# A written instruction order, half as many start-up products of ones and a reordered first batch in a packed-attention and ELU feed-forward kernel

## Chip, core and metric

The kernel runs on one core of a Trainium2 chip. The metric is device microseconds of one execution; the time before is the median of 3 runs. The engines are TensorE (PE; its weight loads are PEld), VectorE (DVE), ScalarE (ACT), GpSimd (POOL) and SyncE (SP), which here only issues DMAs.

## What is computed

Eight batches of eight heads attend twice through 32 packed rows per head, and the result goes through a feed-forward layer with ELU:

```python
def sm_attn(qq, kk, vv):
    s = scale * np.matmul(qq, kk.transpose(0, 1, 3, 2))
    s = s - np.max(s, axis=-1, keepdims=True)
    a = np.exp(s)
    a = a / (np.sum(a, axis=-1, keepdims=True) + 1e-09)
    return np.matmul(a, vv)
p_packed = sm_attn(p, k, v)
out = sm_attn(q, p_packed, p_packed)
...
h = x @ w_in
g = np.where(h > 0.0, h, alpha * (np.exp(np.minimum(h, 0.0)) - 1.0))
return (g @ w_out).astype(np.float32)
```

Here q, k and v are 8 x 8 x 576 x 64, p is 8 x 8 x 32 x 64, w_in is 512 x 2048, w_out is 2048 x 512, and x is the attention output as 4608 tokens of 512.

## The kernel before, in words

**Attention of a batch.** `attention(b, ts)` loads packed rows p, keys, values and queries. `s1` (L588) multiplies keys by p; `smax1` and `sexp1` (L599, L605) are the first softmax; `tr1` (L695) transposes its result on TensorE and four copies by the helper of L377 bring it back; `pv` (L721) multiplies it by the values, 40 small products for both groups of heads (g = 0 and 1); `norm` (L733) divides, `tr2` (L747) transposes, `tr2c` copies: that is ppT, the packed values. `s2` (L770) multiplies ppT by the queries, in two halves of 288 tokens. The second softmax is then a chain of steps over 128 x 576 elements of one half: `fold` (L778), `smax`, `ssub`, `sexp` (on ScalarE), `ssum`, `srec`, `smul`, `unfold` (L822). Its result is called a.

**Feed-forward.** The attention output is never formed: `mstep` (L886) multiplies ppT by w_in into a matrix m (copied from PSUM by the L377 helper as m_hi, its remainder m_lo by L899), and h = a times m. For the first batch's first 512 columns of w_in this product is plain float32 (L1420); elsewhere it is three products of high and low parts (L1427, L1146). Then ELU, a split of the result into g (cast on L377, remainder by L1469 or L1237), and the product with w_out (L1542 to L1545 in batches 0 and 1; L1306 in later batches, where pairs of blocks are combined by sums on L1228 first, so that fewer products are needed). The weights arrive in 64-bit words: a load `raw` (L408), a cast `tops` (L377), a `join` (L426), and for w_out a split in high and low. Four `raw` buffers go round.

**What sets the order.** Every piece of work is an `op` with a priority, the engines that may do it with a cost each, dependences and buffers. `schedule()` (L220) walks a clock of its own over those costs and grants engines and buffers; the order in which it grants them is the order in which instructions are written, so each engine runs its queue in exactly that order. `Ring` and `Banks` say when buffers and PSUM banks come free. `FIRST` (L101) orders the first loads.

**Products of ones.** `warm_up` (L380) multiplies a tile of ones into a PSUM bank nobody reads. It runs with `N_WARM` = 14 (L107) ahead of everything, 20 more `op`s of two can fill idle time (`N_FILL`, L108), and `schedule()` puts further ones behind a TensorE op where the clock shows a gap, up to the first dense product. 63 run in all, 22 of them ahead of `s1`.

**The end.** Accumulators of the last two blocks are added into the tiles kvq and part on VectorE (L1338) and stored.

## Time and profile before

| | |
|---|---|
| median of 3 runs | 659.95 us (659.65 to 660.55) |
| profiled execution, first to last instruction | 657.06 us |
| median less that span | 2.89 us |
| PE busy | 646.5 us, 98% of the span |
| DVE, ACT, POOL busy | 513.0, 421.5, 99.0 us |
| DMA, whole span | 140.50 MB, mean 214 GB/s |

The times are of whole executions; the profile has one execution's span, and no time of its own for what lies around it. A timeline row reads: start, length, engine and line, operation, output and input tiles, shapes, count, and in brackets how long the engine was idle before and what ended that. TensorE's products are pipelined, so "busy" there means that products are in flight.

### The profile page before, as it was taken

How to read it: one execution, taken by the hardware profiler on the slowest of the kernel's cores; microseconds unless marked ns; L12 is line 12 of the kernel's file. 1: busy time of each engine (PE TensorE's matmuls, PEld its weight loads, DVE VectorE, ACT ScalarE, POOL GpSimd, SP SyncE). 2: the span in 40 equal slices, each digit the busy share in tenths (PEclk: the TensorE clock that was granted, in tenths of full speed). 3: DMA queues.
4: the chain of work that ended last, by engine and by line, in shares of the span. 5: the costliest groups of instructions: out<-in, count | busy, mean ns of one | idle time of the engine just before them, and what ended most of it. 6: DMA issues, size and time to landing. Idle time of an engine off the chain costs nothing.

```text
span 657.1 us, 15842 instructions
## 1 busy us (share of the span) xinstructions
PE 646.5 (98%) x6049; PEld 571.1 (87%) x6049; DVE 513.0 (78%) x1083; ACT 421.5 (64%) x839; POOL 99.0 (15%) x133
## 2 busy tenths in 40 slices
PE   9999999999999999999999999999999999999996
PEld 4567888898789989898998997999989998999996
DVE  2878755999988897767986768758997778778885
ACT  4798898777775666655675555765566567555451
POOL 1245466211210010000201000001110002000000
PEclk9999999999999999999999999999999999999999
DMA  8896761787949666583678484547867155775873
GB/s 334 320 334 214 268 234 46 214 248 216 259 138 303 214 210 211 183 252 133 224 253 280 127 255 127 165 129 250 274 225 240 47 169 170 221 229 178 302 228 129
DMA packets 88108, 140.50 MB, mean 214 GB/s; under 512 B 24544, under 2 KB 34272, under 8 KB 87776
## 3 DMA queue, kind: packets, MB, share of 16 engines
q1 hardware_dynamic: 86304, 136.34, 63.7%
q0 software_dynamic: 1440, 2.62, 2.4%
q8 instruction: 48, 0.79, 0.5%
q10 hardware_dynamic: 288, 0.52, 0.2%
q14 instruction: 28, 0.23, 0.1%
HBM read 114.81 MB, written 24.64 MB: 212 GB/s over the span
## 4 chain that ended last, share of the span: by engine, by line
PE 90%; ACT 4%; DVE 4%; issue 1%; DVEq 0%; ACTq 0%
PE psum L1306 42%; PE psum L1146 22%; PE psum L1427 5%; PE psum L886 4%; PE psum L1542 3%; PE psum L1545 3%; PE psum L1543 3%; PE psum L384 2%; PE psum L721 1%; PE psum L770 1%; PE psum L695 1%; PE psum L1420 1%; ACT tops L377 1%; ACT e L1445 1%; ACT e L1451 1%
## 5 line engine op out<-in xcount | busy, mean ns | idle before, releaser
L1306 PE MATMUL psum<-sw,g 128*128 128x256 f32 x936 | 132.7, 276 | 0.0
L1306 PEld LDWEIGHTS psum<-sw,g 128*128 128x128 f32 x936 | 118.3, 192 | 1.9 <-issue 0.8
L1237 DVE TENSOR_TENSOR g<-w,g 128x896 fp32r<-128x896 f32 (+1 forms) x96 | 91.1, 950 | 26.8 <-ACT g L377 26.1
L1146 PE MATMUL psum<-a_hi,m_hi 128*128 128x256 f32 (+1 forms) x384 | 111.6, 291 | 0.1
L1146 PE MATMUL psum<-a_lo,m_hi 128*128 128x256 f32 (+1 forms) x384 | 110.2, 287 | 0.0
L1146 PE MATMUL psum<-a_hi,m_lo 128*128 128x256 f32 (+1 forms) x384 | 110.2, 287 | 0.0
L377 ACT CAST g<-w 128x896 fp32r<-128x896 f32 (+1 forms) x96 | 78.4, 821 | 48.5 <-PE psum L1306 21.2
L1306 PE MATMUL psum<-wo_b,g 128*128 128x256 f32 (+1 forms) x675 | 106.5, 298 | 0.0
L1306 PEld LDWEIGHTS psum<-wo_b,g 128*128 128x128 f32 x675 | 93.4, 191 | 6.1 <-issue 2.2
L1306 PE MATMUL psum<-wo_a,g 128*128 128x256 f32 (+1 forms) x591 | 95.8, 297 | 0.0
L1306 PEld LDWEIGHTS psum<-wo_a,g 128*128 128x128 f32 x591 | 81.3, 191 | 8.7 <-issue 4.4
L1146 PEld LDWEIGHTS psum<-a_hi,m_hi 128*128 128x128 f32 x384 | 73.2, 191 | 3.6 <-issue 0.9
L1146 PEld LDWEIGHTS psum<-a_lo,m_hi 128*128 128x128 f32 x384 | 73.3, 191 | 0.5
L1158 ACT ACTIVATE e<-psum 128x320 f32<-128x320 f32 x96 | 41.4, 432 | 49.9 <-PE psum L1146 49.0
L1146 PEld LDWEIGHTS psum<-a_hi,m_lo 128*128 128x128 f32 x384 | 73.2, 190 | 0.0
L1153 DVE SCALAR_TENSOR_TENSOR w<-e,psum 128x256 f32<-128x256 f32 x96 | 40.0, 416 | 28.4 <-ACT e L1161 27.8
L1228 POOL TENSOR_TENSOR w<-w 128x128 f32<-128x128 f32 (+1 forms) x41 | 23.3, 568 | 248.9 <-DVE w L1153 117.8
L1158 ACT ACTIVATE w<-psum 128x512 f32<-128x512 f32 x48 | 28.7, 599 | 43.6 <-PE psum L1146 28.6
L1228 DVE TENSOR_TENSOR w<-w 128x256 f32<-128x256 f32 (+1 forms) x145 | 49.4, 341 | 2.2
L1161 ACT ACTIVATE e<-e 128x320 f32<-128x320 f32 x96 | 45.0, 471 | 2.6
L1153 DVE SCALAR_TENSOR_TENSOR w<-w,psum 128x512 f32<-128x512 f32 x48 | 32.5, 678 | 15.7 <-ACT w L1161 15.3
L899 DVE TENSOR_TENSOR m_lo<-psum,m_hi 128x1024 fp32r<-128x1024 f32 (+1 forms) x38 | 37.7, 1015 | 2.7 <-ACT m_hi L377 2.6
(123 smaller groups left out, 1188.1 us busy)
## 6 DMA issues: line engine op xcount, KB each, us to landing
sw<-sw_dram SPq DMA_DIRECT2D x248, 256.0 KB, 3.9
kvq<-in_v SPq DMA_DIRECT2D x16, 512.0 KB, 5.2
sw_dram<-sw SPq DMA_DIRECT2D x32, 256.0 KB, 3.9
raw<-in_w_out SPq DMA_DIRECT2D x16, 511.8 KB, 5.3
raw<-in_w_in SPq DMA_DIRECT2D x16, 511.8 KB, 5.7
kvq<-in_kT SPq DMA_DIRECT2D x14, 576.0 KB, 5.3
kvq<-in_qT SPq DMA_DIRECT2D x14, 576.0 KB, 5.5
out<-part SPq DMA_DIRECT2D x28, 256.0 KB, 3.8
```

The source lines that it names most:

```text
L377: (nc.scalar.copy if e == "ACT" else nc.vector.tensor_copy)(out=out, in_=in_)
L886: nc.tensor.matmul(ps.t[cols_of(pair), g, :w], lhsT=st.ppT.t[rows_of(g), pair, :], rhs=w_in_sb[rows_of(g), pair, c * FC + part * w:c * FC ...
L899: nc.vector.tensor_tensor(out=m_b[1].t[:, :, fs], in0=ps.t[:, :, :w], in1=m_b[0].t[:, :, fs].bitcast(F32), op=ALU.subtract,)
L1146: nc.tensor.matmul(ps, lhsT=m_b[p].t[:, g, o:o + P], rhs=in_turn(st.a.t[q][:, g, cols]), start=(n == 0), stop=(n == 3 * G - 1),)
L1153: nc.vector.scalar_tensor_tensor(out=out, in0=e_, scalar=-1.0, in1=ps, op0=ALU.add, op1=ALU.max)
L1158: nc.scalar.activation(out=out, in_=ps, func=AF.Relu, scale=-1.0)
L1161: nc.scalar.activation(out=x, in_=x, func=AF.Exp, scale=-1.0)
L1228: eng(e).tensor_tensor(out=out, in0=x, in1=y, op=o)
L1237: nc.vector.tensor_tensor(out=g_b.all[:, 7 * P:(7 + b1 - b0) * P], in0=blocks(b0, b1), in1=g_b.all[:, :(b1 - b0) * P].bitcast(F32), op=ALU ...
L1306: nc.tensor.matmul(a.t[:, at * H:(at + rhs.shape[1]) * H], lhsT=operand(blk, p), rhs=rhs, start=new and n == k == 0, stop=a.final == (u, m ...
L1427: nc.tensor.matmul(ps_b.t[:, :n_tok], lhsT=m_b[x].t[:, g, o:o + P], rhs=in_turn(st.a.t[y][:, g, cols]), start=(n == 0), stop=(n == 3 * G - 1),
L1542: nc.tensor.matmul(a.t, lhsT=g_b.t[0][:, t], rhs=w[0], start=first, stop=False)
```

## The change

1. **First loads.** The p of batch 0 is issued from ScalarE's queue. The queries of batch 0 come in two loads, of 256 and 320 tokens. `FIRST` names keys, values, first queries, then weights; the written order decides in the end.
2. **Products of ones.** `N_WARM` is 11, `N_FILL` 0, and a table `ONES` says how many follow which op: 13 ahead of `s1`, 36 in all. The memset of the ones covers half the tile and stands first on VectorE.
3. **Value product.** In batch 0 `pv` is two ops, one for each head group, each waiting for its own two copies.
4. **Second softmax.** In batch 0 its two parts are of 256 and 320 tokens, not 288 and 288, and the first waits for the first query load alone.
5. **A written order.** `schedule()`, `Ring.grant` and `Banks.places` are gone. `ORDER` lists all ops with an engine letter where there is a choice, and `PLACES` the PSUM bank of each; dependences stay and are still waited for. Costs given to `op` change too, but no longer decide anything.

```diff
+ORDER = """
+2 1 7 416 417A 0 8 9 10 14 11 403 404V 405 12 17 13 15A 16A 18A 3 4 19A 20 400 5 22A 418 21 23V 24
+25A 408 401V 402 26 406V 6 27 28 29 409A 410 37 407G 48 55 529 30 31 424 425A 32 33 34 426 530A 733
...
+PLACES = (
+    "462626066252064324016426346264562456720412121043201162304343030040371030416061024640015621523016"
...
+ONES = {0: 2, 8: 7, 21: 1, 26: 7, 529: 8}
...
+    CUTS = slice(0, 2 * P), slice(2 * P, S)
...
-    FIRST = "k o0 i1 o1 q v i0 i2 i3".split()
+    FIRST = "k0 v0 v1 q0 i0 i1 q1 o0 i2 i3 o1".split()
...
-    N_WARM = 14
-    N_FILL = 20
+    N_WARM = 11
+    N_FILL = 0
...
-    def schedule():
...
+    nc.vector.memset(part_sb[:, 0, :E // 2], 1.0)
     nc.vector.memset(ebias, -1023.0 * LN2)
...
-    nc.vector.memset(part_sb[:, 0, :], 1.0)
...
-                nc.sync.dma_start(out=q_b[0].t, in_=qT[b])
+                cs = CUTS[n]
+                nc.sync.dma_start(out=q_b[0].t[:, :, cs], in_=qT[b, :, :, cs])
...
-            nc.sync.dma_start(out=p_b.t, in_=pT[b])
+            (nc.sync if b else nc.scalar).dma_start(out=p_b.t, in_=pT[b])
...
-        o = op(ts[2], {"PE": 1.19}, pv, ld_v + tr_done, take=[ps, pp_b], use=v_b + e1T, mode=2)
+        if b == 0:
+            o = op(
+                ts[2], {"PE": 0.65}, lambda e: pv(e, [0]), ld_v + tr_done[:2], take=[ps, pp_b],
+                use=v_b + e1T[:1], mode=2,
+            )
+            pvs = [o, op(
+                ts[2], {"PE": 0.65}, lambda e: pv(e, [1]), tr_done[2:], use=[ps, pp_b] + v_b + e1T[1:],
+                mode=2, after=[o],
+            )]
...
+            cs = CUTS[half] if b == 0 else slice(half * HS, (half + 1) * HS)
+            w = cs.stop - cs.start
...
     with tc.manual_schedule():
-        for o, e in schedule():
+        for x in ORDER.split():
+            o = ops[int(x.rstrip("PVAG"))]
+            e = on_name[x[-1]] if x[-1] in on_name else next(iter(o.on))
+            assert e in o.on and seen.issuperset(d.n for d in o.deps + o.after)
+            seen.add(o.n)
             for buf in o.take:
+                if isinstance(buf.ring, Banks):
+                    buf.at = int(next(places))
                 buf.t = buf.make()
             o.fn(e)
-            if o.ones > 0:
-                warm_up(e, o.ones)
+            if o.n in ONES:
+                warm_up(e, ONES[o.n])
```

The order moves instructions all over the program. Three places follow, each as it stood and as it stands. The first is SyncE's queue from its first load on; k0 and q0 are the first batch's keys and queries, kvq its values, raw a weight, p packed rows.

```order
L560 DMA p_132<-in_pT 128x128
L533 DMA k0_134<-in_kT 128x2304
L408 DMA raw_141<-in_w_out 128x2047
L408 DMA raw_165<-in_w_in 128x2047
L408 DMA raw_173<-in_w_out 128x2047
L542 DMA kvq_185<-in_v 128x2x512
L546 DMA kvq_185<-in_v 64x256
L542 DMA kvq_205<-in_v 128x2x512
L546 DMA kvq_205<-in_v 64x256
L552 DMA q0_220<-in_qT 128x2304
L408 DMA raw_274<-in_w_in 128x2047
L408 DMA raw_292<-in_w_in 128x2047
```

After the change the same stretch of SyncE's queue reads:

```order
L583 DMA k0_118<-in_kT 128x2304
L458 DMA raw_123<-in_w_in 128x2047
L458 DMA raw_175<-in_w_out 128x2047
L592 DMA kvq_193<-in_v 128x2x512
L596 DMA kvq_193<-in_v 64x256
L592 DMA kvq_196<-in_v 128x2x512
L596 DMA kvq_196<-in_v 64x256
L458 DMA raw_221<-in_w_in 128x2047
L603 DMA q0_223<-in_qT 128x4x256
L458 DMA raw_252<-in_w_in 128x2047
L603 DMA q0_223<-in_qT 128x4x320
L611 DMA p_290<-in_pT 128x128
```

Packed rows leave this queue; three weights that stood ahead of the values become two; the queries are cut, and their first 256 tokens stand behind three weights, as the whole did, one of which now follows the values. In both kernels the second batch's keys come behind the same loads: all of the first batch, the same six weights, and that batch's p.

The second is ScalarE, from the copy of the first batch's packed values (ppT) to the first cast of a. tmp is the second softmax's tile, where ACTIVATE is its exponential; m_hi is the first part of m.

```order
L377 COPY ppT_277<-psum_95 128x128
L377 CAST wo_a_107<-mi_272 128x512
L377 CAST tops_114<-raw_274 128x512
L377 CAST tops_114<-raw_292 128x512
L796 ACTIVATE tmp_283<-tmp_283 128x576
L377 CAST tops_114<-raw_308 128x512
L377 COPY m_hi_328<-psum_95 128x2x256
L377 CAST a_hi_363<-k0_355 128x2x288
```

After the change ScalarE reads, between the same two:

```order
L427 COPY ppT_249<-psum_95 128x128
L427 CAST tops_114<-raw_252 128x512
L866 ACTIVATE tmp_256<-tmp_256 128x512
L427 CAST tops_114<-raw_313 128x512
L427 COPY m_hi_293<-psum_95 128x2x256
L427 CAST a_hi_326<-k0_319 128x2x256
```

Two casts ahead of the exponential become one, and one of the last weights stands between the exponential and m_hi in both.

The third is VectorE at the end of the kernel: the last additions into part and kvq.

```order
L1338 TENSOR_TENSOR part_85<-part_85,psum_95 128x256
L1338 TENSOR_TENSOR part_85<-part_85,psum_95 128x2x256
L1338 TENSOR_TENSOR kvq_8877<-kvq_8877,psum_95 128x256
L1338 TENSOR_TENSOR part_85<-part_85,psum_95 128x256
L1338 TENSOR_TENSOR part_85<-part_85,psum_95 128x512
L1338 TENSOR_TENSOR part_85<-part_85,psum_95 128x256
```

After the change VectorE ends with:

```order
L1411 TENSOR_TENSOR part_85<-part_85,psum_95 128x256
L1411 TENSOR_TENSOR part_85<-part_85,psum_95 128x2x256
L1411 TENSOR_TENSOR part_85<-part_85,psum_95 128x256
L1411 TENSOR_TENSOR kvq_8845<-kvq_8845,psum_95 128x256
L1411 TENSOR_TENSOR part_85<-part_85,psum_95 128x512
L1411 TENSOR_TENSOR part_85<-part_85,psum_95 128x256
```

The addition into kvq, which waits for TensorE's last products, stood ahead of three additions into part and stands ahead of two.

On TensorE the second batch's `s1` stands, in both kernels, between the first two blocks' products h and the next two blocks'; it stood behind the second part of m and now stands ahead of it. Elsewhere the counts change by engine: of the 234 block sums (L1228) POOL did 53 and does 126, VectorE did 181 and does 108. The number of products on TensorE other than ones is the same, and so is the number of changes between products of different tile sizes, 140.

## Rows read from the trace of the kernel before

**Rows 1.** Stretches: length, busy PE, PEld, DVE, ACT, POOL; PE clock, DMA share, GB/s

```profile
0.00:25.20 25.20, 22.91 (x234) 9.85 (x234) 10.54 (x19) 12.01 (x24) 5.24 (x11) 1.00 0.94 358
25.20:40.00 14.80, 13.13 (x193) 9.78 (x194) 12.87 (x25) 13.77 (x33) 5.18 (x5) 1.00 0.81 273
40.00:60.00 20.00, 19.98 (x187) 14.00 (x186) 16.04 (x33) 18.87 (x44) 11.47 (x12) 1.00 0.91 302
...
100.00:650.00 550.00, 549.87 (x5157) 503.20 (x5156) 443.61 (x948) 341.75 (x659) 57.60 (x84) 1.00 0.65 202
```

**Rows 2.** TensorE timeline, first 30 us: start, length, work, idle before it

```profile
1.48 7.58 PE L384 MATMUL psum<-part 128*128 128x512 bf16 x22 [1.48 <-DVE part L332]
8.99 1.20 PE L588 MATMUL psum<-k,p 64*32 64x288 f32 x32
...
13.29 2.32 PE L384 MATMUL psum<-part 128*128 128x512 bf16 x10
15.54 1.46 PE L721 MATMUL psum<-kvq,tmp 128*32 128x64 f32 x80
...
18.21 1.20 PE L770 MATMUL psum<-q,ppT 64*32 64x288 f32 x32
...
25.24 1.96 PE L1420 MATMUL psum<-k,m_hi 128*128 128x256 f32 x8 [0.40 <-DVE k L822]
...
27.59 1.18 PE L588 MATMUL psum<-kvq,p 64*32 64x288 f32 x32
29.07 1.97 PE L1420 MATMUL psum<-k,m_hi 128*128 128x256 f32 x8 [0.30 <-DVE e L1454]
```

**Rows 3.** DMA view, 1 to 22 us: queues, issues, KB, us to landing

```profile
q8 instruction: 1, 0.02, 0.3%
...
k<-in_kT SPq DMA_DIRECT2D x1, 1152.0 KB, 5.2
q<-in_qT SPq DMA_DIRECT2D x1, 1152.0 KB, 9.9
```

**Rows 4.** DMA view, 3.3 to 22 us: mean rate while the queue is full

```profile
DMA packets 2204, 7.54 MB, mean 403 GB/s; under 512 B 223, under 2 KB 479, under 8 KB 1966
```

**Rows 5.** SyncE timeline, first 42 us: when loads are issued

```profile
1.18 0.42 SPq L533 DMA_DIRECT2D k<-in_kT  x1
...
6.41 0.35 SPq L552 DMA_DIRECT2D q<-in_qT  x1
```

**Rows 6.** Tile raw, issues from 5 to 7.9 us: first load behind the queries

```profile
L408 SPq DMA_DIRECT2D raw<-in_w_in x1: 340/340/340, 7.7 to 7.7; - x1
...
DMA to landing us min/median/max: 11.4/11.4/11.4
```

**Rows 7.** Tile in_kT, issues from 16 to 20 us: second batch's keys

```profile
L535 SPq DMA_DIRECT2D kvq<-in_kT x2: 328/644/960, 17.0 to 17.5; - x2
...
DMA to landing us min/median/max: 6.2/6.7/7.2
```

**Rows 8.** VectorE timeline: first step of batch 0's second softmax

```profile
19.11 0.78 DVE L778 STREAM_TRANSPOSE tmp<-psum 128x576 f32<-128x576 f32 x1 [1.90 <-PE psum L770]
```

**Rows 9.** ScalarE timeline: a weight cast, then the copy the product needs

```profile
22.11 0.78 ACT L377 CAST tops<-raw 128x512 f16<-128x512 bf16 x1
22.90 0.59 ACT L377 COPY m_hi<-psum 128x512 f32<-128x512 f32 x1
```

**Rows 10.** Instructions by line and form, VectorE: block sums

```profile
L1228 DVE TENSOR_TENSOR w<-w 128x128 f32<-128x128 f32 x91 | 26.6, 293 | 1.4
```

**Rows 11.** Instructions by line and form, POOL: block sums

```profile
L1228 POOL TENSOR_TENSOR w<-w 128x128 f32<-128x128 f32 x33 | 16.5, 500 | 223.0 <-DVE w L1153 117.8 <-DVE hb L1153 72.4 <-DVE w L1228 32.5
```

**Rows 12.** Tile w on line 1228 of POOL: shortest, median and longest sum

```profile
L1228 POOL TENSOR_TENSOR w<-w x41: 455/460/1362, 187.4 to 610.9; 128x128 f32<-128x128 f32 x33, 128x256 f32<-128x256 f32 x8
```

**Rows 13.** VectorE timeline, end of the kernel: the last additions

```profile
651.40 0.42 DVE L1338 TENSOR_TENSOR kvq<-kvq,psum 128x256 f32<-128x256 f32 x1
651.73 1.34 DVE L1338 TENSOR_TENSOR part<-part,psum 128x256 f32<-128x256 f32 x3
```

More of the change, by code (lines that the diff above doesn't have):

```diff
@@ L153, in __init__ @@
         def __init__(self, n):
-            self.n, self.taken = n, []
-        def grant(self, bufs, now):
-            for k in range(len(self.taken) - self.n, len(self.taken) - self.n + len(bufs)):
-                if k >= 0 and not self.taken[k].released(now):
-                    return False
-            return True
-        def take(self, bufs, now):
-            self.taken += bufs
-    class Banks:
-        def __init__(self, n):
-            self.held = [None] * n
-        def places(self, bufs, now):
-            free = [h is None or h.released(now) for h in self.held]
-            out = []
-            for b in bufs:
-                at = [i for i in range(0, min(len(free), b.lim), b.n) if all(free[i:i + b.n])]
-                if not at:
-                    return None
-                i = min(at, key=lambda i: (free[i ^ 1], i)) if b.n == 1 else at[-1]
-                free[i:i + b.n] = [False] * b.n
-                out.append(i)
-            return out
-        def grant(self, bufs, now):
-            return self.places(bufs, now) is not None
-        def take(self, bufs, now):
-            for b, i in zip(bufs, self.places(bufs, now)):
-                b.at = i
-                self.held[i:i + b.n] = [b] * b.n
+            self.n = n
+    class Banks(Ring):
+        pass
     class Buf:
@@ L192, in __init__ @@
             self.ring, self.make, self.n, self.users, self.t = ring, make, n, [], None
-            self.free, self.lim = False, 8
-        def released(self, now):
-            self.free = self.free or all(u.end is not None and u.end <= now for u in self.users)
-            return self.free
+            self.at, self.lim = None, 8
     class Op:
@@ L451, in weights @@
         last = op(
-            prio, {"DVE": 0.69}, join, [x], take=take if plain or first else [mi_b],
+            prio, {"DVE": 0.73}, join, [x], take=take if plain or first else [mi_b],
             use=[raw, top_b] + [b for b in words_b if b not in take],
@@ L559, in load_p @@
         def load_p(e):
[L560 removed]
+            (nc.sync if b else nc.scalar).dma_start(out=p_b.t, in_=pT[b])
         lds, prev_ld = {}, prev_b and prev_b.ld_q
[L563 removed]
+        ld_p = op(ts[0] - 6 if b else -1000, {"DMA": 0.3} if b else {"ACT": 0.45}, load_p, take=[p_b], after=[prev_ld], lag=1.5)
         for name, fn, bufs, t in (
@@ L910, in mstep @@
         ready = mstep_done(b, c, part, parts_, prio, ps, m_b, hi, lo_, whole)
-        ready(op(prio, {"PE": 0.86 / parts_}, mm, pre, after=[b >= NB0 and m_last[0] or None],
+        ready(op(prio, {"PE": 0.89 if parts_ == 1 else 0.46}, mm, pre, after=[b >= NB0 and m_last[0] or None],
                  take=[ps] + (m_b if part == 0 else []), use=[st.ppT] + (m_b if part else []), mode=1))
@@ L1365, in strassen_pair @@
             q = i - T_SE
-            y = op(q, {"ACT": 0.45} | ({} if both else {"DVE": 0.4}), first, [acc[0].last], take=[part], use=acc[:1])
+            y = op(q, {"ACT": 0.375} | ({} if both else {"DVE": 0.425}), first, [acc[0].last], take=[part], use=acc[:1])
             y = op(q, {"DVE": 0.42}, add1, [y], use=[part, acc[0]])
```

376 lines of the change are left out of this document (233 added, 143 removed), and 3 rows, old and new, of the table ORDER.

## The prediction

> **What bounds the kernel now.** I read the stretches first [rows 1], for the engine that never rests. From 100 to 650 us TensorE is busy 549.87 of 550.00 us: nothing is to be won there without fewer products, and the change removes none. From 25.2 to 40 us it idles 14.80 - 13.13 = 1.67 us, from 40 to 60 us 0.02 us. The first 25.2 us are another matter: the TensorE timeline [rows 2] shows no dense product before 25.24 us, only the first batch's attention with products of ones between. So each microsecond by which that first dense product comes earlier shortens the kernel, if what follows can keep up.
>
> What held the start? In the timeline the 22 ones run from 1.48 us for 7.58 us, and the product of keys follows at 8.99 with no idle time. The keys were issued at 1.18 and landed 5.2 us later, at 6.4 [rows 3, 5]: the ones held `s1` for 2.6 us. The ten ones at 13.29 likewise run up to the value product at 15.54. The queries were issued at 6.41 and landed 9.9 us later, at 16.3 [rows 3, 5], yet `s2` began at 18.21: attention, not the load, was late. Loads are close behind, though: from 3.3 to 22 us the queue moves 403 GB/s without a pause [rows 4], which is 524,288 / 403,000 = 1.30 us for a piece of 512 KB.
>
> The sum is made against the profiled span, 657.06 us; the 2.89 us to the median of 659.95 are taken as unchanged.
>
> **Part by part.**
>
> *Ones ahead of `s1`.* 22 in 7.58 us, against ten in 2.32 us later [rows 2]. At a late pace of 0.215 us, 22 would take 4.7; the excess of 2.85 is 13 or 14 products at twice that, 0.43. Their spacing is that of 1.2 GHz, then of 2.4 GHz. The 13 that stay take 13 x 0.43 = 5.5 us. The half-size memset, now first, starts them some 0.35 us earlier (0.1 us for the other memset, 0.25 us for half of the ones), so at 1.1 us, and `s1` can start at 6.65 instead of 8.99.
>
> *First loads.* The keys are now SyncE's first load: one issue earlier, 0.45 us (an issue takes 0.42 [rows 5]), so they land at 5.95. The first 256 tokens of the queries stand behind the same three weights as the whole did, but need 640 KB less: 16.3 - 0.45 - 640/512 x 1.30 = 14.2 us. The p load goes to ScalarE's queue, which then has nothing else to do; it costs its 64 KB of the same transfer time, 0.16 us.
>
> *Value product in two.* `s1` to `pv` was 6.55 us with ones between; without the ten ones' 2.3 us it would be about 4.3, so 11.0 us. The values, at 5.95 + (512 + 512 + 1152)/512 x 1.30, land at 11.5 to 12. From `pv` to `s2` it was 18.21 - 15.54 = 2.67. With the first group's norm beside the second group's product, `s2` would start at 14.0 to 14.4. Both sides meet: I take **`s2` at 14.2 us**, 4.0 earlier.
>
> *256 tokens first.* The chain from its first step to the dense product was 25.24 - 19.11 = 6.13 us [rows 2, 8]. Seven passes of 0.78 us over 576 elements lose 64 of them, at most 0.09 us each, so 0.5 us; `s2` to the first step loses 0.1. The dense product could start at 14.2 + 0.8 + 5.6 = 20.6 us.
>
> *What is late next.* First ScalarE: it must cast a weight, then copy m_hi (0.78 and 0.59, [rows 9]), and that weight (i3) comes late. Before, the first 512 KB behind the queries were issued at 7.7 and landed 11.4 us later, at 19.1 [rows 6], though 16.3 + 1.30 = 17.6 would do. One packet of instructions moved on another queue between 1 and 22 us [rows 3]; I read the 1.5 us as one DMA engine held up by it. The second batch's keys, issued at 17.5, landed 7.2 later, at 24.7 [rows 7], with the same delay. After the change the same loads stand ahead of those keys, so they land at 24.7 - 0.45 = 24.2, or at 22.7 without the delay. The weight i3 would land at about 20.1 or 18.6, and the dense product start at 21.5 or 20.6. Four products h take 1.96 us; then TensorE meets `s1` of batch 2, whose keys are in at 24.2: it waits 0.7 us or more. It ran at 27.59. **This wait ends last**, so of the earlier start 27.59 - 24.2 = 3.4 us remain. Its bounds are 2.3 (if the m copy behind it also slips: the next products h at 26.8 for 29.07) and 4.6 (no delay).
>
> *25 to 100 us.* The 1.67 us of waits [rows 1] stand on ScalarE, VectorE and weights. The order is new there, and what it waits for cannot be read from the trace of before. All of it may go, or as much may come; weights have the DMA time, since the queue was busy 0.81 of 25 to 40 us. I take half gone, 0.8, with bounds of 1.7 gained and 1.7 lost.
>
> *The end.* TensorE's last products release an addition into kvq at 651.40, and the three into part last from 651.73 for 1.34 us [rows 13]. One of the three, 0.33 us from start to start, now stands ahead of that wait: 0.3 us saved.
>
> *Sums on POOL.* 73 more of them, at 0.50 us against VectorE's 0.29 [rows 10, 11]. 73 x 0.5 = 37 us more on POOL, which has 57.6 of 550 busy; VectorE has 443.6 of 550. I cost it at nothing: TensorE's full queue covers it, as long as each g is ready before its turn; without cover it costs the 0.21 us difference or more a sum. POOL's sums, of both widths, took 0.46 us in the median and up to 1.36 [rows 12]; I read the long ones as held up by VectorE. The Trainium skill (SBUF — State Buffer, Who interferes with whom) says that a VectorE instruction with two SBUF inputs and a GpSimd one that reads SBUF exclude each other, the later one waiting for the whole of the other; that speaks against this change. By that rule VectorE would lose up to 37 us of waiting and 73 x 0.29 = 21 us of work: 459 of 550, still not the bound, and the sum stays.
>
> Sum: 3.4 + 0.8 + 0.3 = 4.5 us, so 659.95 - 4.5 = **655.4 us**.
>
> **Rivals.**
> - *Loads without the delay, waits gone.* The held-up DMA engine is hit later, the dense part starts 4.6 us earlier, 1.5 of the waits go, 0.3 at the end: 653.5. For it: 27 ones are fewer, so TensorE's instruction packets come later. Against: one such packet in 20 us suffices.
> - *Conversion gives it back.* From 25.2 to 60 us ScalarE is busy 32.64 of 34.80 us [rows 1]. If it is the pace, only its 2.2 us of free time can be saved, and 0.3 at the end: 657.5. Against: several casts and copies go to VectorE, which has 5.9 us free.
> - *POOL makes g late: slower.* Each sum moved lengthens its chain by 0.21 us, and by up to 1.36 - 0.29 = 1.07 where it is blocked. With 73 at a mean of 0.2, some 15 us of lengthening stand against the lead that g has on TensorE. It decides where over 4.5 us of it, a third, outlast that lead; with half, 655.4 + 7.3 = 662.7. Against: TensorE never idled from 100 to 650 us [rows 1].
> - *Clock.* The granted clock is 1.00 (2.4 GHz) in every stretch from 25.2 us [rows 1], with ones in each gap; now 27 ones go and gaps of about a microsecond are left. A fall to 1.2 GHz before the dense part costs what it cost at the start, 13 x 0.215 = 2.8 us: 658.2. The Trainium skill (TensorE: Matmul & The Clock Gate, Part 1) says that idleness puts the clock back to half; no gap here shows it yet.
> - *Nothing much happens.* If the second batch's keys come late by another 3 us, the start is worth nothing: about 659.5.
>
> **How the numbers follow.** Chances: forecast (654.2 to 656.8) 0.47, no delay 0.17, conversion 0.15, POOL 0.09, clock 0.05, nothing 0.07. A measurement tells 0.2%, 1.3 us, from no change, so faster means under 658.6. That holds for the first two, nearly all of the third and most of the fourth case: 0.81. The same: 0.10; slower: 0.09. The range leaves out the POOL case and the upper part of the last, and below goes 0.9 us under the second case for its bounds: 652.6 to 658.6.
>
> **What would show it.** Right: `s1` near 6.7 us, `s2` near 14.2, first dense product at 20.6 to 21.5, `s1` of the second batch at about 24.2 right behind its keys, last addition within 1.5 us of TensorE's end. Wrong: `s1` of the second batch near 27; TensorE idle by more than 2 us from 25 to 100; idle time from 100 to 650 us released by g or by POOL; a granted clock under 1.00 after the start.

## The result, and the profile after

The changed kernel takes 663.41 us (median of 4 runs, 662.81 to 664.2), the kernel before 659.8 us beside it (4 runs, 658.61 to 660.55): ratio 1.0059, 95% interval 1.0044 to 1.0073. It is **slower by 3.6 us** where the prediction had it 4.5 us faster. The profiled execution took 663.94 us, with a span of 662.2.

The stretches of [rows 1], now of the changed kernel (length, busy PE, PEld, DVE, ACT, POOL; PE clock, DMA share, GB/s):

```profile
0.00:25.20 25.20, 21.25 (x237) 9.69 (x245) 13.45 (x27) 11.35 (x24) 3.90 (x10) 0.93 0.96 357
25.20:40.00 14.80, 13.87 (x207) 10.47 (x191) 14.46 (x29) 13.01 (x30) 8.21 (x7) 1.00 0.88 302
40.00:60.00 20.00, 18.41 (x162) 12.81 (x161) 19.93 (x38) 17.39 (x36) 8.29 (x9) 1.00 0.76 258
60.00:100.00 40.00, 37.62 (x256) 31.86 (x255) 37.02 (x78) 31.20 (x69) 13.49 (x13) 1.00 0.61 198
100.00:650.00 550.00, 547.57 (x5127) 498.34 (x5125) 432.49 (x865) 334.31 (x640) 132.51 (x175) 1.00 0.65 205
```

The engine that never rests is now VectorE: 19.93 of 20.00 us from 40 to 60, 37.02 of 40 behind. TensorE, which stood still for 0.02 us from 40 to 60 and 0.13 from 100 to 650 [rows 1], stands still for 1.59 and 2.43 us. POOL's time behind 100 us has gone from 57.60 to 132.51 us.

TensorE's timeline, as [rows 2]:

```profile
1.18 4.88 PE L434 MATMUL psum<-part 128*128 128x512 bf16 x13 [1.18 <-DVE ebias L380]
7.21 1.20 PE L643 MATMUL psum<-k,p 64*32 64x288 f32 x32 [1.15 <-POOL p L710]
...
11.59 2.08 PE L776 MATMUL psum<-kvq,tmp 128*32 128x64 f32 x80
...
15.23 1.11 PE L837 MATMUL psum<-q,ppT 64*32 64x256 f32 x16 [0.67 <-DMA q<-in_qT]
16.27 2.88 PE L434 MATMUL psum<-part 128*128 128x512 bf16 x7
19.55 0.77 PE L837 MATMUL psum<-q,ppT 64*32 64x320 f32 x16 [0.40 <-DMA q<-in_qT]
...
22.42 1.89 PE L1493 MATMUL psum<-k,m_hi 128*128 128x256 f32 x8
24.24 1.58 PE L643 MATMUL psum<-kvq,p 64*32 64x288 f32 x28
...
27.43 1.99 PE L1493 MATMUL psum<-k,m_hi 128*128 128x256 f32 x8 [0.93 <-ACT m_hi L427]
```

The first dense product (L1493, before L1420) starts at 22.42 for 25.24, the second batch's `s1` (L643) at 24.24 for 27.59. Not all of that is gain: this `s1` now runs ahead of the second part of m, which took 0.46 us of TensorE before it (27.13 to 27.59). The next products h are the first place where both kernels have the same work behind them. They start at 27.43 for 29.07, after a wait for the m_hi copy: there **1.6 us** of the head's gain are left.

**Where the lead goes.** The span shows only the end, so I compared the two traces product by product. Each TensorE `op` starts at a known time in each trace; the table costs of the ops started before it, summed, say how far the program is; the two times at equal progress differ by the lead. Left, the time in the kernel before; minus means ahead, in us. Every column is one profiled execution; e1 and e2 are the runs with engines put back, low_v, f_lows and so on those described under the same names below.

```
time   after  e1    e2   low_v f_lows f_sp f_ones f_all  m75  m180  m520 best520 sumsG best150 best434
  28   -3.5  -3.9  -2.1  -2.1  -2.3  -3.9  -4.1  -3.9  -2.1  -3.4  -3.9  -3.8  -4.0  -3.6  -3.4
  44   -4.0  -1.9  -2.6  -2.5  -2.6  -4.3  -4.5  -4.2  +1.8  -3.8  -4.3  -4.2  -4.3  -4.3  -3.7
  60   -2.0  -0.6  -0.6  -1.7  -1.8  -2.2  -2.5  -3.4  +1.8  -0.5  -2.1  -2.8  -3.4  -0.1  -1.9
  84   -2.2  +3.2  -0.9  -1.9  -1.9  -2.4  -2.7  -3.6  +1.8  -0.1  -2.3  -3.0  -3.6  -0.3  -2.1
 102   +0.2  +6.5  +0.3  +0.5  -1.3  -0.4  -1.5  -2.9  +1.8  +0.1  +0.2  -1.7  -2.1  +0.4  +1.0
 147   +0.9  +7.4  +1.0  +1.2  -0.6  +0.3  -1.0  -2.2  +2.9  +0.1  +4.1  +2.1  +1.9  +1.5  +1.0
 291   +2.3  +7.8  +3.2  +2.5  +0.8  +3.5  +0.4  -1.7  +3.0  +0.2  +4.2  +2.4  +3.2  +1.5  +1.1
 578   +3.1  +7.9 +13.9  +2.8  +1.2  +4.0  +0.8  -0.2  +3.0  +0.6  +4.2  +2.4  +4.5  +1.8  +1.3
 638   +4.2  +8.9 +15.9  +3.6  +2.5  +4.1  +0.9  -0.1  +3.0  +0.6  +4.4  +2.4  +5.4  +1.9  +1.3
```

The first row stands inside the swapped `s1` and m, so it reads too high. Where both kernels have started exactly the same products, the changed kernel is ahead by 2.8 us at the first dense product, 1.6 at 29 us, 2.3 at 36, 3.5 at 42, 1.6 at 44 and 82, and behind by 0.9 at 105 and 4.8 at the last product. The table's later rows are some 0.6 us more favourable than that, and their falls are the same within 0.3 us. So the changed kernel gains 1.6 us in its head and some 2 more by 42 us, where waits of the kernel before are gone; it gives back 4.2 us between 44 and 102 us and 4.0 us more behind. The columns e2, low_v, f_lows and m75 start lower for the clock's sake (*Ones and the clock*). (The span grew by 5.1 us, the medians by 3.6: the profiled execution of after was one of its slower ones, that of before, as far as its span tells, one of its quicker ones.) The longest waits of TensorE, without those of the first 20 us (waits: who waited for whom; us in total, times, longest):

```profile
PE psum L837 <- DVE w_in_sb L476: 1.6, 1, 1.6
PE psum L1500 <- DVE e L1527: 1.3, 2, 0.8
...
PE psum L1379 <- DMA sw<-sw_dram: 1.0, 2, 0.8
```

No wait is long. I had three theories: **V**, VectorE took over work of ScalarE and GpSimd in 25 to 100 us and is the pace there; **S**, the sums of g on GpSimd cost the time behind 100 us; **W**, it is the written order itself, whatever the engines. A fourth, **B**, came from the trace: VectorE and GpSimd keep each other waiting.

### The profile page after: what moved, and what is told of

Read it like the earlier page. It is cut to its first block, busy times and chain, and to the rows that moved or that the text cites. A ratio compares the mean times of both kernels' runs of the same rounds, so it can differ in the third digit from the quotient of the medians.

```text
span 662.2 us, 15833 instructions
## 1 busy us (share of the span) xinstructions
PE 644.9 (97%) x6022; PEld 569.2 (86%) x6022; DVE 523.4 (79%) x1045; ACT 408.4 (62%) x797; POOL 166.4 (25%) x213
## 4 chain that ended last, share of the span: by engine, by line
PE 77%; DVE 10%; DMA 6%; ACT 3%; issue 2%; SPq 1%; DVEq 0%; ACTq 0%
PE psum L1379 40%; PE psum L1219 21%; PE psum L959 4%; PE psum L1500 3%; DMA raw<-in_w_in 2%; DMA sw<-sw_dram 2%; PE psum L1615 2%; PE psum L1618 2%; PE psum L1616 2%; DVE e L1527 1%; PE psum L776 1%; DMA kvq<-in_v 1%; DVE w_in_sb L476 1%; PE psum L837 1%; ACT tops L427 1%
## 5 line engine op out<-in xcount | busy, mean ns | idle before, releaser
L1301 POOL TENSOR_TENSOR w<-w 128x128 f32<-128x128 f32 (+1 forms) x104 | 75.3, 727 | 327.8 <-DVE w L1226 137.8
L1379 PE MATMUL psum<-wo_a,g 128*128 128x256 f32 (+1 forms) x591 | 93.9, 295 | 0.0
L1231 ACT ACTIVATE e<-psum 128x320 f32<-128x320 f32 x96 | 41.5, 432 | 61.6 <-PE psum L1219 58.6
L1226 DVE SCALAR_TENSOR_TENSOR w<-e,psum 128x256 f32<-128x256 f32 x96 | 38.4, 415 | 15.5 <-ACT e L1234 15.2
L1542 POOL TENSOR_TENSOR g<-e,g 128x256 fp32r<-128x256 f32 x34 | 29.7, 879 | 47.3 <-DVE g L427 24.1
```

What stands on the lines that cost most here:

```text
L1226: nc.vector.scalar_tensor_tensor(out=out, in0=e_, scalar=-1.0, in1=ps, op0=ALU.add, op1=ALU.max)
L1231: nc.scalar.activation(out=out, in_=ps, func=AF.Relu, scale=-1.0)
L1301: eng(e).tensor_tensor(out=out, in0=x, in1=y, op=o)
L1379: nc.tensor.matmul(a.t[:, at * H:(at + rhs.shape[1]) * H], lhsT=operand(blk, p), rhs=rhs, start=new and n == k == 0, stop=a.final == (u, m ...
L1542: eng(e).tensor_tensor(out=g_b.t[1], in0=e_b.t[:, own], in1=g_b.t[0].bitcast(F32), op=ALU.subtract)
```

## Experiments

In the diffs, an entry of `ORDER` is an op's number and a letter for its engine: V VectorE, A ScalarE, G GpSimd.

**Engines put back.** First the two edits that leave the order and change engines only.

```diff
+BACK = """
+63A 64A 69A 111A 414A 422A 468A 478A 479G 486A 492A 494A 495G 511G 518A 519G 526A 527G 751A 758A
+766G 818A 835A 856G 862A 863G 869A 870G 877G 883A 884G 890A 891G 898G 904A 917G 926G 933A 950A
+"""
...
+        back = {x[:-1]: x for x in BACK.split()}
         for x in ORDER.split():
+            x = back.get(x.rstrip("PVAG"), x)
```

> The changed kernel's written order as it stands, but 39 of its entries between 25 and 100 us go back to the engine that they have in the kernel before: casts (top, high, cast, norm, tr1a, tr1b) from VectorE to ScalarE, subtractions (low, sub_own) from VectorE to GpSimd. Theory V (VectorE took over some 12 us of ScalarE's and GpSimd's work in 25 to 100 us and became the pace there; the changed kernel's lead of 3.5 us at 44 us is gone at 100): 660.0 to 661.5, and the lead at 100 us is 2 us or more. Rival S (the sums of g on GpSimd, later, are the loss): 663.4, no change. Rival W (it is the order, not the engine; in an order written for other engines the work then waits elsewhere): 663 or slower.

Measured: 668.68 us, ratio 1.0154 (1.0127 to 1.0182): 5.3 us slower than the changed kernel by the medians, 6.3 by the ratios. From 60 to 100 us VectorE falls to 23.77 us, yet TensorE stands still for 3.99:

```profile
60.00:100.00 40.00, 36.01 (x240) 29.88 (x238) 23.77 (x45) 33.05 (x75) 19.86 (x22) 1.00 0.57 183
```

Its longest waits from 25 to 104 us end on ScalarE now:

```profile
PE psum L1504 <- ACT tops L431: 1.4, 1, 1.4
PE psum L780 <- ACT tmp L431: 1.2, 1, 1.2
PE psum L963 <- ACT tmp L664: 1.1, 1, 1.1
```

That is rival W's range: V, as "the engines were chosen badly", is out; in this order VectorE is the better place for that work. The other edit is the same with 129 sums in `BACK` (`1300V 1316V 1317V ...`).

> The changed kernel with the 129 sums of g that changed their engine put back on the engine of the kernel before (101 from GpSimd to VectorE, 28 the other way), nothing else. Theory V: 663.4, since nothing changes ahead of 100 us. Rival S: from 100 us on the changed kernel loses about 3.4 us against the kernel before, and its GpSimd has 132 us of work there for 58; if the sums are that loss, 660 to 661.5. If the written order alone loses it: 663 to 665.

Measured: 676.05 us, ratio 1.0257 (1.0235 to 1.0279), 12.6 us slower. The lead falls from -0.9 at 84 us to +15.9, most of it behind 291 us; no expectation reaches so far. The longest waits from 140 us on are for VectorE's ELU (L1237), in whose queue 73 more sums now stand:

```profile
PE psum L1230 <- DVE w L1237: 4.0, 5, 2.3
PE psum L1390 <- DVE w L1237: 1.2, 2, 0.7
```

S, as a fault that one could undo, is out too. In this order both groups of engine choices are better than those of the kernel before.

**The old planner behind the new head.** `schedule()`, `Ring` and `Banks` of the kernel before are back, with most of its costs; the first entries are forced, 75 of them in the first run and 480 in the second.

```diff
+HEAD = """
+2 1 7 416 417A 0 8 9 10 14 11 403 404V 405 12 17 13 15A 16A 18A 3 4 19A 20 400 5 22A 418 21 23V 24
...
+"""
...
+            for n, o in enumerate([head[len(out)][0]] if len(out) < len(head) else todo[:400]):
...
-        for x in ORDER.split():
+        for o, e in schedule():
```

> The changed kernel's code and the first 75 entries of its written order (to 27 us: loads, ones, first attention, first dense products), then the kernel before's planner with its costs for the rest. If the head's gain of 3.3 us is real and everything behind it (engines, order) gives it back: 655.5 to 657. If the gain can't survive, since the conversion of weights holds the pace whatever the order: 659 to 660.5.

> The same with the first 480 entries (to 100 us), then the planner. Theory V and a second loss behind 100 us of about 3.4 us: as far as 100 us it is the changed kernel (level with the kernel before), from there the kernel before: 659.3 to 660.5. If everything is lost ahead of 100 us and no order can mend it: 663. If the first 100 us cost nothing: 656 to 657.

Measured: 675.55 us (1.0244, 1.0222 to 1.0266) and 669.41 us (1.0163, 1.0143 to 1.0183). Both miss every expectation. The planner does not return to the order it made before: a few op costs and a head that differ are enough for another plan, 2.4% slower than the old one in h75. These two runs say nothing of the head; they say that "the planner" is no fixed point of comparison. From here on I wrote the order of the kernel before out, entry by entry, with its engines and banks.

**Seams.** The first N entries of the changed order, then the work that is left in the order of before. m75 and m180 have N in their names; r100 turns it round, the order of before up to 100 us and the changed one behind. The diff at N = 75:

```diff
-745G 49 50 56 57 432 433A 59 40 531 532A 747 754 58
...
+411 412 413 414 415G 49 50 432 440 531 40 532 56 41
...
```

> The changed kernel's code and written order for the first 75 entries (to 27 us); behind them the order, engines and banks of PSUM in which the kernel before runs the same work, written out, so that no planner plans anew. Measured by the product that stands at the same place, the changed kernel is 3.5 us ahead at 28 us and 4.0 at 44 us, and 0.2 behind at 102 us. If the head's lead is real and it is the changed kernel's order behind it that loses it: 655.5 to 657. If the lead can't be kept (the weights come no earlier): 659 to 660. If the order of before only suits its own head: slower than 660.

> The same with the first 180 entries of the changed kernel's order (to 44 us, where its lead is largest) and the order of before behind them. If the losses start at 44 us: 655 to 656.5, a little ahead of the run with 75. If the changed order to 44 us has only borrowed its lead from work put off until later: 657.5 or slower.

> The other way round: the order, engines and banks of the kernel before up to 100 us, the changed kernel's order behind (its code throughout). Behind 102 us the changed kernel loses 4.0 us more, bit by bit (0.8 by 130, 2.6 by 330, 1.1 at 590). If that loss is in the later order and its engines, whatever came first: 662.5 to 664.5. If the later losses come from what the first 100 us leave behind: 659.5 to 660.5.

Measured: m75 661.66 us (1.0033, 1.0015 to 1.0052), m180 660.18 us (1.0022, 1.001 to 1.0035), r100 677.46 us (1.0279, 1.0255 to 1.0304). m75 and m180 come out in the slowest of their cases, r100 beyond both of its own. The columns m75 and m180 say more: the lead is lost at the seam (m75 behind 28 us, m180 between 44 and 60), and then next to nothing happens for 500 us (m75 loses another 1.1 by 147 us). r100 lost 7.0 us at its seam and 10.8 behind it; a bad seam, a bad order and a clock of 0.66 from 105 to 115 us are not told apart in it. TensorE in m75 around the seam, then the wait there:

```profile
21.16 2.81 PE L425 MATMUL psum<-part 128*128 128x512 bf16 x7 [0.33 <-issue]
23.81 1.89 PE L1484 MATMUL psum<-k,m_hi 128*128 128x256 f32 x8
...
30.10 3.65 PE L1484 MATMUL psum<-k,m_hi 128*128 128x256 f32 x8 [2.84 <-ACT m_hi L418]
```

ScalarE at that place:

```profile
28.95 0.62 ACT L418 CAST wo_a<-mi 128x512 fp32r<-128x512 f32 x1 [0.81 <-DVE mi L467]
29.47 0.58 ACT L418 COPY m_hi<-psum 128x512 f32<-128x512 f32 x1
```

The m_hi copy stands behind a cast that waits for a join on VectorE: a piece of w_out that the changed order converts later. The seam is not alone in m75's column: the clock reads 0.66 from 20 to 25 and from 30 to 35 us, and the eight products at 30.10 take 3.65 us, for 1.99 in the changed kernel. Two of its ten executions, at mean clocks of 0.999 and 1.0, took 658.18 and 658.40 us, as much as the quickest of the kernel before (658.23).

**GpSimd and VectorE.** VectorE and then POOL of the changed kernel at 85 us:

```profile
85.67 1.71 DVE L476 SCALAR_TENSOR_TENSOR w_in_sb<-raw,tops 128x512 uint32<-128x512 uint32 x1 [0.49 <-ACT tops L427]
87.30 1.47 DVE L1542 TENSOR_TENSOR g<-e,g 128x256 fp32r<-128x256 f32 x1
88.69 0.68 DVE L972 TENSOR_TENSOR m_lo<-psum,m_hi 128x512 fp32r<-128x512 f32 x1
```

```profile
85.42 3.06 POOL L490 TENSOR_TENSOR wo_b<-mi,wo_b 128x512 fp32r<-128x512 f32 x2
```

Two subtractions of a weight's low part run on POOL from 85.42 to 88.48. A join on VectorE takes 1.71 us for some 0.7, a subtraction 1.47 for 0.42. TensorE then waits for m_lo and e until 91.02. Two more such subtractions stand at 36 and 41 us; the first edit moves these.

```diff
-68 70A 69V 768 435 436A 759G 44 45 71 456 459 72A 753 763 764 769 457A 770 551 552 431G 760 437 438A
-460A 771 553 557 765A 53 73 458 779 787 772A 461 558 766V 559 74 448 449A 439G 767 450 443 780 75
+68 70A 69V 768 435 436A 759G 44 45 71 456 459 72A 753 763 764 769 457A 770 551 552 431V 760 437 438A
+460A 771 553 557 765A 53 73 458 779 787 772A 461 558 766V 559 74 448 449A 439V 767 450 443 780 75
```

> The changed kernel with two subtractions of the weights' low parts (entries 431 and 439, 36 and 41 us) on VectorE for GpSimd. At 40.8 and 42.4 us two joins on VectorE took 1.70 and 1.22 us, where others take 0.68, while GpSimd ran one of these, and the lead fell from 4.0 to 2.1 us. If VectorE waits for GpSimd's subtractions there (theory B): the joins take 0.7 us again for 0.68 us of subtraction each, the lead at 47 us is 2.5 to 3.5, and the time 662.5 to 663.4. If VectorE is simply full there (theory V): the lead at 47 us is 2 or less, and the time 663.4 to 664.5.

Measured: 662.85 us, ratio 1.0058 (1.0043 to 1.0074). By its time inside B's range; the lead did not fall from 44 to 48 us, but this execution came later to the place, with a slow clock in its head, and by 102 us its lead is gone as in the changed kernel. Not settled by this run. With the other pair too (`503V`, `487V`):

> The changed kernel with four subtractions of low parts (entries 431, 439, 503, 487) on VectorE for GpSimd. In its trace the VectorE instruction that meets each of them waits: joins of 1.70 and 1.22 us at 40.8 and 42.4 us, one of 1.71 at 85.7 and a subtraction of 1.47 at 87.3, where 0.68 and 0.42 are usual; TensorE then waits for VectorE at 42.6 (1.55 us), 88.7 and 89.9 us (1.5). Theory B (VectorE and GpSimd keep each other waiting, and VectorE has no slack there): 1.0 to 2.0 us less than the changed kernel, ratio to before 1.003 to 1.0045. Theory V (VectorE full, whoever subtracts): no gain, ratio 1.005 to 1.007.

Measured: 661.71 us, ratio 1.0034 (1.0021 to 1.0047), 1.7 us less than the changed kernel; the two intervals overlap barely. From 84 to 102 us it loses 0.6 of its lead, where low_v and the changed kernel lose 2.4. VectorE at the same place:

```profile
85.54 0.71 DVE L476 SCALAR_TENSOR_TENSOR w_in_sb<-raw,tops 128x512 uint32<-128x512 uint32 x1
86.17 0.41 DVE L1542 TENSOR_TENSOR g<-e,g 128x256 fp32r<-128x256 f32 x1
86.50 0.68 DVE L490 TENSOR_TENSOR wo_b<-mi,wo_b 128x512 fp32r<-128x512 f32 x1
87.10 0.68 DVE L972 TENSOR_TENSOR m_lo<-psum,m_hi 128x512 fp32r<-128x512 f32 x1
```

VectorE does one step more and is done with m_lo 1.6 us earlier. B holds at 85 us. At 42 us something else comes first: the page's first wait, "L837 <- DVE w_in_sb", is `s2` of the second batch, which reads queries and ppT and no w_in_sb. The tile in_qT of the changed kernel, issues from 30 to 50 us, and its TensorE row; then the same product in best434, where the join is done at 41.5:

```profile
L605 SPq DMA_DIRECT2D kvq<-in_qT x2: 576/577/578, 35.9 to 44.1; - x2
...
DMA to landing us min/median/max: 6.5/6.5/6.6
```

```profile
42.55 0.72 PE L837 MATMUL psum<-kvq,ppT 64*32 64x288 f32 x16 [1.55 <-DVE w_in_sb L476]
```

```profile
42.75 0.72 PE L828 MATMUL psum<-kvq,ppT 64*32 64x288 f32 x16 [1.52 <-DMA kvq<-in_qT]
```

Issued at 35.9, landed 6.5 later, at 42.4: it is the load. The changed order runs this `s2` early and lets it depend on a load that lands between 39.9 us (f_ones) and 42.6 us (best434). Where the load is in time, B shows behind it. In f_ones `s2` ran at 40.40, beside the long join (1.70 us from 40.28), and TensorE then waited for VectorE:

```profile
47.19 1.05 PE L1493 MATMUL psum<-k,m_hi 128*128 128x320 f32 x3 [1.15 <-DVE hb L1527]
```

f_ones lost 2.0 us of its lead between 44 and 60 us, as much as the changed kernel. f_all (below), which has the subtractions on VectorE as well, waits for nothing from 38 to 62 us and loses 0.8. So the load and B stand there one behind the other.

**SP's queue.**

```diff
-1384G 169V 1397 1398 171 1420 172A 1421 1422 147 1351 1352 1353 1385V 1399 1400V 1401G 1386 1364
-1365 1387 1425 1366 1426 1427 1424 1430 1431G 173 148 1367 1368 1432G 1369 1370 1377 1423 174 175
+1384G 169V 1397 1398 171 1420 172A 1421 1422 1351 1352 1353 1385V 1399 1400V 1401G 1386 1364
+1365 1387 1425 1366 147 1426 1427 1424 1430 1431G 173 148 1367 1368 1432G 1369 1370 1377 1423 174 175
...
-2831 2840 2832 2833 2917 2834 2845 2846 2847 2863 2844 2875 2858 2864 2892 2918 2919 2920 2921 2871G
+2831 2840 2832 2833 2917 2834 2845 2846 2847 2863 2844 2858 2875 2864 2892 2918 2919 2920 2921 2871G
```

> The changed kernel with two DMA issues moved on SP's queue: entry 147, a load of queries that waited 9.2 us for TensorE with three sums of weights behind it (issued 210.1 us, product late by 0.9 us at 215.9), behind these three; entry 2858, a store of leftover rows that stood behind a load waiting until 583.2 us (product late by 1.0 us at 587.4), ahead of that load. If these head-of-line waits are part of the loss behind 102 us: 1.3 to 2.0 us less than the changed kernel, ratio to before 1.003 to 1.004. If something else is as late at both places: ratio 1.005 to 1.007.

Measured: 663.19 us, ratio 1.0061 (1.0049 to 1.0073): nothing gained. The changed kernel's waits at 205 to 232 and at 575 to 600 us, and what f_sp has in their place at 266 to 300:

```profile
PE psum L1379 <- DMA sw<-sw_dram: 0.8, 1, 0.8
...
PE psum L1219 <- DVE w L1226: 0.8, 1, 0.8
```

```profile
PE psum L1379 <- DMA sw<-sw_dram: 1.1, 1, 1.1
```

Both waits are gone, and the lead at 638 us is the same: another load of sums is late 70 us on.

**Ones and the clock.**

```diff
-ONES = {0: 2, 8: 7, 21: 1, 26: 7, 529: 8}
+ONES = {0: 2, 8: 7, 21: 1, 26: 15, 529: 8}
```

> The changed kernel with 15 products of ones behind the second softmax's first scores for 7: TensorE stands idle from 17.3 to 19.3 us there, and the granted clock reads 0.66 to 0.69 in a stretch of 5 us behind it in three of four profiles of this head (1.00 throughout in the kernel before, which runs 63 products of ones in its first 25 us, this one 36). If the clock's fall costs time: every run at a mean clock of 0.998 or more, 0.7 to 1.5 us less than the changed kernel's median, ratio 1.0035 to 1.005. If it costs nothing, since the engine waits for loads there: ratio 1.005 to 1.007.

Measured: 662.1 us, ratio 1.0049 (1.0032 to 1.0066), 0.7 us less than the changed kernel by the ratios, whose intervals overlap. Mean clocks of its runs are 0.995 to 0.999, not 0.998 or more: half a miss, though its profile, at a mean of 0.997, has 1.00 up to 650 us and 0.78 behind, where TensorE is nearly done. What the clock does is plain in m75, 20 to 25 us, beside f_ones:

```profile
20.00:25.00 5.00, 4.67 (x36) 2.28 (x18) 4.04 (x6) 2.52 (x5) 0.00 (x0) 0.66 1.03 418
```

```profile
20.00:25.00 5.00, 4.84 (x55) 2.88 (x56) 4.53 (x9) 4.30 (x9) 0.03 (x1) 1.00 1.02 419
```

TensorE of f_ones, beside the rows of m75 above:

```profile
15.45 3.41 PE L434 MATMUL psum<-part 128*128 128x512 bf16 x15
18.96 0.77 PE L837 MATMUL psum<-q,ppT 64*32 64x320 f32 x16
...
20.32 1.67 PE L434 MATMUL psum<-part 128*128 128x512 bf16 x7 [0.16 <-issue]
21.83 1.89 PE L1493 MATMUL psum<-k,m_hi 128*128 128x256 f32 x8
```

In m75 TensorE idled 2.03 us ahead of 19.30; the next seven ones took 2.81 us (1.2 GHz) for 1.67, and the first dense product came at 23.81 for 21.83. The runs whose head is the changed kernel's, entry by entry, price the fall. First dense product of e1, whose clock reads 1.00 from 15 to 25 us, and of f_lows, which has 1.00 from 15 to 20 and 0.66 from 20 to 25:

```profile
22.05 1.89 PE L1497 MATMUL psum<-k,m_hi 128*128 128x256 f32 x8
```

```profile
23.70 1.89 PE L1493 MATMUL psum<-k,m_hi 128*128 128x256 f32 x8
```

That is 1.65 us; e2 and low_v are as late (23.84 and 23.81). In the changed kernel's own profile the clock fell earlier, 0.66 from 15 to 20 us, and that cost little: `s2` behind the slow ones still waited 0.40 us for its queries, and the dense product came at 22.42. And m75's ten executions run from 658.18 us at a mean clock of 0.999 to 663.57 at 0.992.

**All edits.** f_lows, f_sp and f_ones together.

> All three edits together. If the three losses are separate: 3 to 5 us less than the changed kernel, 658.5 to 660.5, ratio to before 0.9985 to 1.0015. If one loss stands behind another: 661 to 662, ratio 1.002 to 1.004.

Measured: 660.33 us, ratio 1.0027 (1.0017 to 1.0037), 2.1 us less than the changed kernel: between the two expectations. It has 2.9 us of its lead left at 102 us and then loses 2.8 (its profile is of its quickest execution, 659.77 us).

**The later order.** Seams at 105 us, with the changed head plain (m520) and mended (best520: the four subtractions and the ones), with the sums' engines changed on top (`1300` on GpSimd for `1300V`, and 128 more), and at 168 us.

```diff
-646A 647G 649A 652A 969 987 1000 984A 978 655A 909V 650G 656V
...
+108 909 910 987 969 984 988 985G 989 1000 992 978 990 993
...
```

> The changed kernel's written order for 520 entries (to some 105 us), then the order, engines and banks of the kernel before, written out. At 105 us the changed kernel is 0.2 us behind the kernel before. If its later order loses the 4.0 us behind: ratio to before 0.999 to 1.002. If the first 105 us leave something behind that costs later: 1.003 to 1.006.

> The same with the four subtractions on VectorE and 15 ones for 7; the run with all edits was 2.9 us ahead at 102 us and level at the end. If the later order is the loss: 655.5 to 657 us, ratio to before 0.995 to 0.998, faster than both kernels. If not: ratio 0.999 to 1.002.

> best520 with the engines of the changed kernel for the 129 sums of g that changed (101 on GpSimd for VectorE, 28 the other way), in the order of the kernel before. Rival S (sums on GpSimd are late for g and hold TensorE): 2 us or more above best520. If the sums' engine is free of cost: within 0.5 us of best520. If it helps, since VectorE has 100 sums less to do: below best520.

> best520 with the seam at entry 888 (some 168 us), where the two orders differ in fewer entries. The run with all edits was 2.2 us ahead there. If the order behind the seam decides: 656 to 657.5, a little above best520. If the order between 105 and 168 us is what loses: at least 1 us above best520.

Measured: m520 663.07 us (1.0055, 1.0034 to 1.0077), best520 661.65 (1.0045, 1.0027 to 1.0063), best520_sumsG 664.9 (1.0087, 1.0069 to 1.0106), best888 666.36 (1.0111, 1.0091 to 1.0131). best520 reaches neither of its cases, and m520 and best888 meet a slow case for a reason that I had not named: the seams cost 3.9, 3.8 and 6.6 us. best520_sumsG meets rival S. Behind the seams the columns settle what was asked. With the order of before, the lead changes by 0.3 us from 147 to 638 us in m520 and best520. With the changed order it falls by 3.3 over the same work. And in best520_sumsG it falls by 3.5, so the sums on GpSimd, alone, cost 3.2 us there, and 3.25 us of the median: S's price is true of that order, though undoing it in the other one was worse. How the sums cost it is not shown: the longest wait there ends on ScalarE's `norm`, none on GpSimd:

```profile
PE psum L802 <- ACT pp L788: 1.1, 1, 1.1
```

The stretch 140 to 640 us of before, of the changed kernel, and of best520_sumsG:

```profile
140.00:640.00 500.00, 499.87 (x4682) 458.37 (x4682) 403.86 (x857) 307.18 (x575) 42.20 (x70) 1.00 0.67 208
```

```profile
140.00:640.00 500.00, 498.00 (x4648) 454.97 (x4647) 386.39 (x768) 302.40 (x565) 113.05 (x153) 1.00 0.66 207
```

```profile
140.00:640.00 500.00, 497.06 (x4637) 454.12 (x4637) 381.00 (x783) 306.16 (x578) 88.44 (x140) 1.00 0.67 205
```

TensorE idles 0.13 us before, 2.00 after. Idle time undercounts a wait, since products in flight cover its first 0.16 us or so: by the distances between the starts of products, the five waits behind those 2.00 us held TensorE up by 2.8 us, and two waits by 0.5 in the kernel before. That leaves about 1 us of the 3.3 in small delays, and what they are stays open.

**Keeping the lead.** Two last seams, where the two orders differ least (entry 150) and where no entry has to move (434).

```diff
-112 515 936 516A 517 523 933V 479V 945 518V 507 519V 524A 923
...
+98 99 108 850 520 566 521 479G 567 568 522 936 923 507
...
```

> The changed kernel's code, 15 products of ones for 7 behind the second softmax's first scores, its written order for 150 entries (to some 37 us; there the two orders differ in the fewest entries), behind it the order, engines and banks of the kernel before. With these ones the lead at 40 us was 4.9 us. If the seam costs 1 to 2 us and the order behind it keeps the rest: 655.5 to 657.5, ratio to before 0.995 to 0.998, faster than both kernels. If the lead is lost between 40 and 70 us as in m180 (3.6 us there): 658.5 to 660, ratio 0.999 to 1.002; then no run shows the head's gain at the end.

> The changed kernel's code, the four subtractions on VectorE, 15 ones for 7, its written order for 434 entries (to some 90 us), then the order, engines and banks of the kernel before, without a single entry moved at the seam. The run with all edits was 3.9 us ahead at 90 us. If the later order is what loses the lead: 656 to 658 us, ratio to before 0.996 to 0.999. If the lead at 90 us is borrowed from conversions put off until later, which before's order then makes up at the seam: 659 to 661, ratio 1.000 to 1.003.

Measured: best150 660.21 us (1.0021, 1.0011 to 1.0031) and best434 661.68 us (1.0047, 1.0031 to 1.0062). Both end a little beyond the slower of their two cases. best150 loses its 4.3 us between 44 and 54 us; best434 loses 3.2 between 90 and 97, in one wait:

```profile
PE psum L1491 <- ACT part L418: 3.0, 1, 3.0
```

By the medians no run beats the kernel before; the two nearest are m180 and best150, at 0.2% above it.

## Why the prediction was wrong

*Ones ahead of `s1`, first loads, value product, 256 tokens first: the forecast time came out, by luck, and half of the gain did not.* I forecast `s1` of the second batch at 24.2 us and it ran at 24.24. On the way most steps were later than forecast. `s1` came at 7.21 for 6.65: p, costed at 0.16 us of transfer, landed 5.8 us after its issue beside the keys, for 1.7 ahead of them before, and POOL's scaling of it ended last. `s2` came at 15.23 for 14.2, behind its queries; the first dense product at 22.42 for 20.6 to 21.5, with ScalarE's cast of a late weight and its m_hi copy ahead of it, as I had named them (20.84 to 22.05). This lateness, 0.9 us, used up the wait of 0.7 us that I had put at `s1`; the keys landed at 23.5 and 24.8, and 0.5 us of that wait stands inside `s1`, ahead of its second half of keys.

**"Of the earlier start 27.59 - 24.2 = 3.4 us remain" is mis-sized.** It takes for gain the 0.46 us of m that `s1` now overtakes, and it ends too early: what holds TensorE next is the m_hi copy, as in my lower bound. The products h behind it, forecast at 26.8 in that bound, came at 27.43 for 29.07: 1.6 us are gained, less than the bound of 2.3. No run tests my reading of the 1.5 us delay as a held-up DMA engine.

***25 to 100 us: "I take half gone, 0.8, with bounds of 1.7 gained and 1.7 lost". This step failed.*** Up to 42 us it does better than forecast: the waits of the kernel before go, and the lead grows from 1.6 to 3.5 us. Then 4.4 us are lost: at 105 us, with the same work done, the changed kernel is 0.9 us behind. From 29 us on that is 2.5 lost where the bound said 1.7. I bounded a whole new order by the idle time of the old one, as if at worst the waits could double (and I left out the 0.76 us that the kernel before idles from 60 to 100). TensorE now idles 4.9 us from 25 to 100 us for 2.45. What stood there instead, as far as the runs show: an `s2` that waits 1.55 us for a load (1.9 lost at 44 us), and VectorE without slack, where mutual waits with GpSimd cost 1.7 us (f_lows). The rival *conversion gives it back* had the place right and the engine wrong: it put the pace on ScalarE and called VectorE's free 5.9 us the argument against; 5.5 of those 5.9 us are what was spent.

***"Sums on POOL ... I cost it at nothing", and with it everything behind 100 us. This step failed too.*** I looked at the sums alone, and at a full TensorE as their cover. Behind 102 us the lead falls by 4.0. The sums on GpSimd cost 3.2 us where nothing else changes (best520_sumsG), so "nothing" was wrong; "POOL makes g late" was the rival, at 662.7 the nearest to the result, with a chance of 0.09. But it is not the whole mechanism, and that the sums make g late is not shown: in the changed order they are better on GpSimd by 12.6 us. That the later order loses is shown, since the order of before keeps the lead over the same work within 0.3 us (m520, best520). How it loses is only in part: in waits of under 1 us on late loads and late ELUs, which came back elsewhere in the one run that mended two of them (f_sp). Which of its choices makes them late stays open.

*The rule on shared access* (the Trainium skill, SBUF — State Buffer, Who interferes with whom) says that a VectorE instruction with two SBUF inputs and a GpSimd one that reads SBUF exclude each other for the whole of the first. The trace agrees: a join of 1.71 us beside GpSimd's subtraction (85.67), 0.71 without it (f_lows). I applied it to the sums behind 100 us, where VectorE had room, and not to the subtractions of weights ahead of 100 us, where it had none.

*Clock.* I gave a fall 0.05 and a price of 2.8 us. Where it fell just ahead of the dense part, with the same head, it cost 1.65 us there (f_lows against e1). In the changed kernel's profile it fell earlier; seven ones took 1.2 us longer, mostly in the shadow of a load. Of the changed kernel's four executions, two at a mean clock of 0.999 took 662.81 and 662.88 us, two at 0.996 and 0.995 took 663.94 and 664.2. The quicker pair is still 3 us behind the kernel before, so the clock is not what lost; f_ones puts its share of the 3.6 us at about 0.7, no more than the intervals allow to be told from nothing.

*The end.* Forecast 0.3 us saved. From the start of TensorE's last product to the end of the span it is 6.3 us for 6.0: none saved. The addition that moved ahead ran until 656.6 us, so the one into kvq started 0.34 us after the end of the last product (656.53 for 656.19), where it was 0.04 us before: what was saved behind it was spent ahead of it.

## What to carry to other kernels

A lead at the start is worth what the order behind it can keep: price a new order over its whole length, with bounds of several us on both sides, not by the idle time of the old one. Compare two traces at equal progress, not at equal time, to see where a lead is lost, and at places where exactly the same work is done, or a swapped pair of steps reads as a gain. And do not judge an engine's assignment apart from the order it was written for: by the medians, putting work back on its old engine cost 5.3 and 12.6 us, planning it anew behind the same head 12.1.

## What the runs showed of the hardware

The granted clock of one program differs from one execution to the next: m75's ten have mean clocks from 0.992 to 1.0 and spread over 5.4 us, the kernel before's 19 beside them, with 63 products of ones, 0.998 to 1.0 and 1.1 us. Gaps of nearly the same length were followed by either level: TensorE idled 1.89 us ahead of 19.17 us in e1 and the clock stayed at 1.00, 2.02 us ahead of 19.19 us in f_lows and it read 0.66 from 20 to 25 us. And a load of 576 KB issued at the same place landed 4.6 us after its issue in f_ones and 6.5 in the changed kernel, which is enough to make a wait of 1.5 us appear or vanish.
